# Masked query copies on GpSimd beside VectorE's PSUM reads, and query projections 40 score rows earlier, in an attention and feed-forward kernel

## Chip, cores, metric

One core of one Trainium2 chip. The metric is device time in microseconds of the whole program, the median of several runs; the lower the better. Every kernel ran in rounds with the kernel before, on the same chip in the same job; where kernels of two jobs are set against each other, their ratios to before are given. All runs used here are in the fast state. One thing still differs among fast runs, the granted TensorE clock (1.0 is full speed).

## The reference

```python
xn = layernorm(x)                                   # x: 1 x 2048 x 512, bf16
q, k, v = heads(xn @ wqkv)                          # 32 heads of 16
o = softmax(q @ k.T * 16 ** -0.5) @ v
out = x + o @ wo + (silu(xn @ w1) * (xn @ w3)) @ w2 # F = 1792
```

## The kernel before

The program is ordered when it is built. A list scheduler in the kernel has a duration for every instruction, steps time in 0.02 us, and emits work for each engine when its operands should be ready. Whatever it decides is fixed: on the chip each engine runs its own list in order and waits on semaphores. Its clock at the end of planning is called the **planned end** below: 786.0 us for the kernel before, 782.6 for the changed one. It is not a time of the chip.

Scores come in tiles of two banks of PSUM (the memory that TensorE writes; SBUF is the one that the other operands lie in), 1024 tiles in all (2048 "score rows", two per tile; a unit of queries has 64 rows). A tile's exponential is made on ScalarE, or on VectorE from a PSUM read ("p1") and four bit operations on pairs of tiles. Two units share one projected query tile: the even heads of it serve one unit, the odd heads the other, each with the rest masked to zero.

```python
def tile_QT(qc, i):
    u0 = qc * NG + 2 * i
    s0, s1 = u0 % 4, (u0 + 1) % 4                   # ring of four query slots
    ...                                             # 4 groups of projection matmuls into the "dense bank", the PSUM bank of projections and feed-forward
    def evac(bk, o, rel):
        def emit():
            q = P.op("dve", ... tensor_scalar(QT[:, s1, :], bank(bk), QS, None, ALU.mult), dur=d_cost(512))
            rel(q)
            q = P.op("dve", ... tensor_scalar(QT[:, s0, :], QT[:, s1, :], msk[:, 0:1], None, ALU.mult), dur=s_cost(512))
            done[("QTm", u0)] = q.end + _LAT        # scores of unit u0 may start
            q = P.op("dve", ... tensor_scalar(QT[:, s1, :], QT[:, s1, :], msk[:, 1:2], None, ALU.mult), dur=s_cost(512))
            done[("QTm", u0 + 1)] = q.end + _LAT
        P.post("dve", emit, ready=o.end + _LAT, prio=1)
...
crit.append((max(1, (qc * NG + 2 * i) * RPU - 60), k, tile_QT(qc, i)))   # begin 60 score rows ahead
```

GpSimd already had one job: the two 256-wide normalisation pieces of a head pair (`e5h`), which the scheduler emits beside a p1 (`beside_p1`) once their DMA should have landed.

## Time and profile before

| | |
|---|---|
| time | 798.39 us, median of 3 (798.28 to 800.65) |
| span of the profiled execution | 795.3 us, granted clock 0.996 |
| busy | ScalarE 772.0, VectorE 768.8, TensorE 750.3, GpSimd 38.0 us |
| exponential tiles | 798 on ScalarE, 226 on VectorE |
| masked copies | 30 on VectorE, 0.27 us each start to start |

The busy shares say that two engines are full; the start-to-start times in a timeline say what an instruction really costs, since neighbours overlap; the bracket at the end of a timeline line says how long the engine sat idle before it and who ended that. The lines themselves are in the prediction.

### The profile page before, as it was taken

How to read it: one execution, taken by the hardware profiler on the slowest of the kernel's cores; microseconds unless marked ns; L12 is line 12 of the kernel's file. 1: busy time of each engine (PE TensorE's matmuls, PEld its weight loads, DVE VectorE, ACT ScalarE, POOL GpSimd, SP SyncE). 2: the span in 40 equal slices, each digit the busy share in tenths (PEclk: the TensorE clock that was granted, in tenths of full speed). 3: DMA queues.
4: the chain of work that ended last, by engine and by line, in shares of the span. 5: the costliest groups of instructions: out<-in, count | busy, mean ns of one | idle time of the engine just before them, and what ended most of it. 6: DMA issues, size and time to landing. Idle time of an engine off the chain costs nothing.

```text
span 795.3 us, 21182 instructions
## 1 busy us (share of the span) xinstructions
PE 750.3 (94%) x9169; PEld 227.6 (29%) x9169; DVE 768.8 (97%) x1039; ACT 772.0 (97%) x872; POOL 38.0 (5%) x60
## 2 busy tenths in 40 slices
PE   8999999999899999999999999998999998999997
PEld 6332222222222222222222222222222222222223
DVE  8899999999999999999999999999999999999993
ACT  5999999999999999999999999999999999999994
POOL 3100201000010000000000000000100000000000
PEclk9999999999999999999999999999999999999989
DMA  7024033331322222233311234322223341332221
GB/s 213 2 23 118 5 35 42 36 34 36 48 35 30 30 36 48 34 48 53 45 17 15 37 47 59 49 33 45 28 22 36 54 60 22 51 35 23 22 15 33
DMA packets 83568, 32.91 MB, mean 41 GB/s; under 512 B 72073, under 2 KB 79753, under 8 KB 83465
## 3 DMA queue, kind: packets, MB, share of 16 engines
q1 hardware_dynamic: 83464, 31.46, 27.6%
q8 instruction: 74, 1.21, 0.6%
q14 instruction: 30, 0.24, 0.1%
HBM read 22.81 MB, written 2.10 MB: 31 GB/s over the span
## 4 chain that ended last, share of the span: by engine, by line
ACT 63%; DVE 23%; PE 12%; issue 1%; DVEq 0%; ACTq 0%
ACT f_PT L1847 60%; DVE f_xd L1920 8%; PE ps L1330 4%; DVE f_xd L1969 4%; PE ps L1784 4%; PE ps L2038 3%; DVE f_xd L1962 2%; ACT f_th L1544 2%; DVE f_xd L1978 2%; DVE f_xd L1984 2%; DVE f_hT L1558 2%; DVE f_t L1548 1%; PE ps L1217 1%; DVE f_U L2056 1%; DVE f_QT L1458 0%
## 5 line engine op out<-in xcount | busy, mean ns | idle before, releaser
L1847 ACT ACTIVATE f_PT<-ps 128x1024 bf16<-128x1024 f32 x798 | 747.6, 1138 | 4.4 <-PE ps L1784 3.7
L1784 PE MATMUL ps<-f_QT,f_KT 32*128 32x512 bf16 x2048 | 310.8, 386 | 26.6 <-ACT f_PT L1847 20.4
L1920 DVE TENSOR_SCALAR f_xd<-ps 128x1024 int16<-128x1024 f32 x226 | 275.1, 1217 | 3.0 <-PE ps L1784 2.7
L2038 PE MATMUL ps<-f_PT,f_Vaug 128*17 128x512 bf16 (+1 forms) x1596 | 210.0, 386 | 3.4 <-DVE f_U L2056 2.2
L2038 PE MATMUL ps<-f_xd,f_Vaug 128*32 128x512 bf16 (+1 forms) x1356 | 182.3, 385 | 3.9 <-DVE f_xd L1969 1.6
L1784 PEld LDWEIGHTS ps<-f_QT,f_KT 32*128 32x128 bf16 x2048 | 79.6, 91 | 323.0 <-ACT f_PT L1847 259.8
L1330 PE MATMUL ps<-f_xnT,f_w 128*32 128x512 bf16 x1792 | 139.9, 384 | 3.0 <-DVE f_t L1548 1.2
L1969 DVE TENSOR_TENSOR f_xd<-f_xd 128x2048 bf16<-128x2048 bf16 x113 | 137.3, 1215 | 0.0
L1962 DVE TENSOR_SCALAR f_xd<-f_xd 128x2048 int16<-128x2048 int16 x113 | 80.5, 713 | 2.7 <-PE ps L2038 1.9
L1984 DVE TENSOR_SCALAR f_xd<-f_xd 128x2048 int16<-128x2048 int16 x113 | 78.0, 690 | 0.0
L1978 DVE TENSOR_SCALAR f_xd<-f_xd 128x2048 int16<-128x2048 int16 x113 | 77.6, 687 | 0.0
L1330 PE MATMUL ps<-f_w,f_hT 128*32 128x512 bf16 x896 | 73.0, 383 | 0.2
L2038 PEld LDWEIGHTS ps<-f_PT,f_Vaug 128*17 128x17 bf16 (+1 forms) x1596 | 51.0, 92 | 63.7 <-issue 45.8
L2038 PEld LDWEIGHTS ps<-f_xd,f_Vaug 128*32 128x32 bf16 (+1 forms) x1356 | 44.5, 92 | 51.3 <-issue 26.9
L2100 POOL TENSOR_TENSOR f_onorm<-f_U,f_R 128x256 bf16<-128x256 f32 x30 | 25.1, 842 | 703.2 <-DMA f_R<-f_Rrow 414.0
L1330 PEld LDWEIGHTS ps<-f_xnT,f_w 128*32 128x32 bf16 x1792 | 36.8, 94 | 62.2 <-issue 51.5
L1544 ACT ACTIVATE f_th<-ps 128x512 f32<-128x512 f32 x56 | 41.0, 733 | 0.0
L1558 DVE SCALAR_TENSOR_TENSOR f_hT<-f_t,ps 128x512 bf16<-128x512 bf16 x56 | 38.0, 679 | 0.4 <-PE ps L1330 0.2
L1548 DVE SCALAR_TENSOR_TENSOR f_t<-f_th,ps 128x512 bf16<-128x512 f32 x56 | 38.0, 678 | 0.3 <-ACT f_th L1544 0.3
L1330 PEld LDWEIGHTS ps<-f_w,f_hT 128*32 128x32 bf16 x896 | 19.3, 95 | 23.7 <-issue 16.3
L2056 DVE COPY f_U<-ps 128x512 f32<-128x512 f32 x31 | 21.2, 685 | 0.4 <-PE ps L2038 0.4
L1330 PE MATMUL ps<-f_wo,f_onorm 128*32 128x512 bf16 x272 | 19.9, 382 | 0.2 <-DVE f_QT L1458 0.2
(81 smaller groups left out, 240.1 us busy)
## 6 DMA issues: line engine op xcount, KB each, us to landing
f_w<-in_B_w_dram SPq DMA_DIRECT2D x112, 128.0 KB, 3.9
f_R<-f_Rrow SPq DMA_DIRECT2D x124, 32.0 KB, 4.1
f_xr<-in_A_x_dram SPq DMA_DIRECT2D x16, 128.0 KB, 2.6
f_U<-f_U SPq DMA_DIRECT2D x60, 32.0 KB, 1.9
f_w<-in_B_w_dram SPq DMA_DIRECT2D x7, 256.0 KB
f_xd<-in_A_x_dram SPq DMA_DIRECT2D x3, 512.0 KB
out_dram<-f_xn_sb SPq DMA_DIRECT2D x12, 128.0 KB
f_xd<-in_A_x_dram SPq DMA_DIRECT2D x2, 256.0 KB
```

Source lines behind the costliest of these rows:

```text
L1330: ins = e.matmul(bank(bk)[32 * i:32 * i + 32, 0:ncols], make_lhsT(i), rhs_ap, start=start, stop=stop, tile_position=(0, 32 * i))
L1544: q = P.op("act", lambda e: e.activation(th[:, ss, :], bank(bk), ACTF.Tanh, scale=0.5), reads=[("ps", bk)], writes=[("th", ss)], dur=a_cos ...
L1548: q2 = P.op("dve", lambda e: e.scalar_tensor_tensor(t1[:, ss, :], th[:, ss, :], 1.0, bank(bk), ALU.add, ALU.mult), reads=[("th", ss), ("ps ...
L1558: q = P.op("dve", lambda e: e.scalar_tensor_tensor(hT[:, fc, :], t1[:, ss, :], 0.5, bank(bk), ALU.mult, ALU.mult), reads=[("t1", ss), ("ps ...
L1784: ins = e.matmul(bank(b), l_, r_, start=True, stop=True, tile_position=(rp, 0))
L1847: q = P.op("act", lambda e: e.activation(PT[:, s_, :], ps[:, b0 * 512:(b0 + 2) * 512], ACTF.Exp, scale=ASC, bias=ABIAS), reads=[("ps", b0) ...
L1920: q = P.op("dve", lambda e: e.tensor_scalar(dsl[:, ys, 1024 * c:1024 * c + 1024], ps[:, b0 * 512:b0 * 512 + 1024], YB, G_LO, ALU.add, ALU. ...
L1962: P.op("dve", lambda e: e.tensor_scalar(dsl[:, NY + m_, 0:n], y, 0x7F, 0x3F00, ALU.bitwise_and, ALU.bitwise_or), reads=YK, writes=[("ds", ...
L1969: q_ = P.op("dve", lambda e: e.tensor_tensor(t_ap.bitcast(BF16), y.bitcast(BF16), t_ap.bitcast(BF16), ALU.mult), reads=YK + [("ds", NY + m ...
L1978: q_ = P.op("dve", lambda e: e.tensor_scalar(g_ap, y, -G_LO, 0.0, ALU.add, ALU.max), reads=YK, writes=[("g", g_, k) for k in range(n // 51 ...
L1984: q_ = P.op("dve", lambda e: e.tensor_scalar(y, y, 0x7F80, None, ALU.bitwise_and), reads=YK, writes=YK, dur=s_cost(n), name="e", lock=True)
L2038: ins = e.matmul(bank(PV)[32 * j:32 * j + (17 if g % 2 == 0 else 32), :], v_, p_, start=s0, stop=s1, tile_position=(0, 32 * j))
```

## The change

Intent: take the two masked copies of each of 15 query tiles off VectorE and give them to GpSimd, in four pieces that run while VectorE reads PSUM and so, by the argument in the prediction, does not need the SBUF port pair that both share; start the projection earlier to leave time for that.

```diff
+    QP_DUR = 0.5
@@ tile_QT, evac
-                    q = P.op("dve", ... QT[:, s0, :] <- QT[:, s1, :] * msk[:, 0:1] ..., lock=True)
-                    done[("QTm", u0)] = q.end + _LAT
-                    q = P.op("dve", ... QT[:, s1, :] <- QT[:, s1, :] * msk[:, 1:2] ..., lock=True)
-                    done[("QTm", u0 + 1)] = q.end + _LAT
+                    P.post("pool", lambda: part(0), ready=q.end + _LAT, prio=1, cond=beside_p1)
+
+                def part(i):
+                    h, cs = i // 2, slice(256 * (i % 2), 256 * (i % 2) + 256)
+                    d_ = (s0, s1)[h]
+                    q = P.op("pool", lambda e: e.tensor_scalar(QT[:, d_, cs], QT[:, s1, cs], msk[:, h:h + 1], None, ALU.mult),
+                             reads=[("QT", s1), ("msk", h)], writes=[("QT", d_)], dur=QP_DUR, name="evQ",
+                             extra=[st["p1_op"]])
+                    if i % 2:
+                        done[("QTm", u0 + h)] = q.end + _LAT
+                    if i < 3:
+                        P.post("pool", lambda: part(i + 1), ready=q.end + _LAT, prio=1, cond=beside_p1)
@@
-                    crit.append((max(1, (qc * NG + 2 * i) * RPU - 60), k, tile_QT(qc, i)))
+                    crit.append((max(1, (qc * NG + 2 * i) * RPU - 100), k, tile_QT(qc, i)))
```

(`beside_p1` moves to where both users see it.)

More of the change, by code (lines that the diff above doesn't have):

```diff
@@ L1427, in tile_D0, with beside_p1 @@
             return out_
+        def beside_p1():
+            return st["p1_at"] == P.t
         def tile_KT(i, sc):
@@ L1460, in emit @@
                     rel(q)
-                    q = P.op("dve", lambda e: e.tensor_scalar(QT[:, s0, :], QT[:, s1, :], msk[:, 0:1], None, ALU.mult),
-                             reads=[("QT", s1), ("msk", 0)], writes=[("QT", s0)], dur=s_cost(512), name="evQ", lock=True)
-                    done[("QTm", u0)] = q.end + _LAT
-                    q = P.op("dve", lambda e: e.tensor_scalar(QT[:, s1, :], QT[:, s1, :], msk[:, 1:2], None, ALU.mult),
-                             reads=[("QT", s1), ("msk", 1)], writes=[("QT", s1)], dur=s_cost(512), name="evQ", lock=True)
-                    done[("QTm", u0 + 1)] = q.end + _LAT
+                    P.post("pool", lambda: part(0), ready=q.end + _LAT, prio=1, cond=beside_p1)
[9 more added lines that the diff above has]
+                        P.post("pool", lambda: part(i + 1), ready=q.end + _LAT, prio=1, cond=beside_p1)
                 P.post("dve", emit, ready=o.end + _LAT, prio=1)
@@ L2092, in e4 @@
                         ("OUT", (u // 2 - NON) // NP * 4 + i) in done for i in range(4))))
-            def beside_p1():
-                return st["p1_at"] == P.t
             def e5h(i):
```

## The prediction

> **What bounds the kernel now.** I read the page's busy shares first, then the forty slices, the chain that ended last, the groups of instructions, and then timelines of VectorE around one query evacuation, of ScalarE over the first 70 us and of GpSimd.
>
> The page of the kernel before:
>
> ```profile
> PE 750.3 (94%) x9169; PEld 227.6 (29%) x9169; DVE 768.8 (97%) x1039; ACT 772.0 (97%) x872; POOL 38.0 (5%) x60
> ACT 63%; DVE 23%; PE 12%; issue 1%; DVEq 0%; ACTq 0%
> L1847 ACT ACTIVATE f_PT<-ps 128x1024 bf16<-128x1024 f32 x798 | 747.6, 1138 | 4.4 <-PE ps L1784 3.7
> L1920 DVE TENSOR_SCALAR f_xd<-ps 128x1024 int16<-128x1024 f32 x226 | 275.1, 1217 | 3.0 <-PE ps L1784 2.7
> L1969 DVE TENSOR_TENSOR f_xd<-f_xd 128x2048 bf16<-128x2048 bf16 x113 | 137.3, 1215 | 0.0
> L1962 DVE TENSOR_SCALAR f_xd<-f_xd 128x2048 int16<-128x2048 int16 x113 | 80.5, 713 | 2.7 <-PE ps L2038 1.9
> L2100 POOL TENSOR_TENSOR f_onorm<-f_U,f_R 128x256 bf16<-128x256 f32 x30 | 25.1, 842 | 703.2 <-DMA f_R<-f_Rrow 414.0
> ```
>
> ScalarE and VectorE are both full, and that is by design: a score tile of 1024 columns gets its exponential either on ScalarE (798 of them) or on VectorE (226, by bit operations; 798 + 226 = 1024). The program is ordered at build time by a list scheduler with its own durations, so freed time on one engine is shared out between both by giving it more tiles. GpSimd is idle at 95%. The chain is ScalarE's exponentials for 60% of the span, with VectorE's 23% mixed in: neither engine alone sets the end. The last 16 us (output projection) contain no query work.
>
> VectorE's timeline around one of the 15 query evacuations:
>
> ```profile
> 190.41 1.22 DVE L1920 TENSOR_SCALAR f_xd<-ps 128x1024 int16<-128x1024 f32 x1
> 191.54 0.68 DVE L1458 TENSOR_SCALAR f_QT<-ps 128x512 bf16<-128x512 f32 x1
> 192.26 0.35 DVE L1461 TENSOR_SCALAR f_QT<-f_QT,f_msk 128x512 bf16<-128x512 bf16 x1
> 192.53 0.35 DVE L1464 TENSOR_SCALAR f_QT<-f_QT,f_msk 128x512 bf16<-128x512 bf16 x1
> 192.79 0.68 DVE L2056 COPY f_U<-ps 128x512 f32<-128x512 f32 x1
> 193.39 0.68 DVE L1984 TENSOR_SCALAR f_xd<-f_xd 128x2048 int16<-128x2048 int16 x1
> ```
>
> Instructions overlap, so starts count, not durations. The masked copies hold VectorE from 192.26 to 192.79. The evacuation takes 0.72 us to the next start, where the same shape without a dependent follower (L2056) takes 0.60.
>
> ScalarE's timeline (30 to 69 us), and VectorE's at the same place:
>
> ```profile
> 30.80 36.90 ACT L1847 ACTIVATE f_PT<-ps 128x1024 bf16<-128x1024 f32 x40
> 69.00 3.77 ACT L1847 ACTIVATE f_PT<-ps 128x1024 bf16<-128x1024 f32 x4 [1.30 <-PE ps L1784]
> ...
> 67.34 0.69 DVE L1458 TENSOR_SCALAR f_QT<-ps 128x512 bf16<-128x512 f32 x1 [0.75 <-PE ps L1330]
> 68.07 0.35 DVE L1461 TENSOR_SCALAR f_QT<-f_QT,f_msk 128x512 bf16<-128x512 bf16 x1
> ```
>
> This is the one place where queries are late. VectorE sat idle 0.75 us for the first query projection, and ScalarE sat idle 1.30 us until scores of the unit using it came. The 40 exponentials also give ScalarE's cost: (36.90 - 1.14) / 39 = 0.917 us per tile.
>
> GpSimd's timeline against VectorE's, where a normalisation piece came late:
>
> ```profile
> 179.35 0.72 POOL L2100 TENSOR_TENSOR f_onorm<-f_U,f_R 128x256 bf16<-128x256 f32 x1 [45.40 <-DVE f_xd L1920]
> 181.30 0.73 POOL L2100 TENSOR_TENSOR f_onorm<-f_U,f_R 128x256 bf16<-128x256 f32 x1 [1.22 <-DVE f_hT L1558]
> ...
> 179.38 1.25 DVE L1962 TENSOR_SCALAR f_xd<-f_xd 128x2048 int16<-128x2048 int16 x1
> 180.55 0.67 DVE L1558 SCALAR_TENSOR_TENSOR f_hT<-f_t,ps 128x512 bf16<-128x512 bf16 x1
> 181.15 1.21 DVE L1920 TENSOR_SCALAR f_xd<-ps 128x1024 int16<-128x1024 f32 x1
> ```
>
> The piece at 179.35 fell beside a 16-bit SBUF operation, whose 0.69 became 1.25. The piece at 181.30 fell 0.15 after the start of a PSUM read (L1920), which stayed at 1.21.
>
> **What the Trainium skill says.** "SBUF — State Buffer", section "Who interferes with whom": VectorE in a 2-port mode contends with GpSimd and whoever issues first blocks the other for the whole instruction, while a VectorE instruction with at most one SBUF input outside these modes does not. The pair of pieces above agrees: +0.56 us in one case, nothing in the other. "VectorE: DVE Perf Modes", section "Why PSUM operands drop a tier", says the 2-port mode is impossible with a PSUM operand, which is why the change pairs its pieces with the PSUM reads. "GPSIMD Engine Reference", section "3.1 Elementwise — side-by-side cycle accounting", gives 1.03 to 1.8 cycles per element at 1.2 GHz for one-input loops; before has no such piece of this width, only a 2-column scalar operation of 0.19 us. "Perfetto Trace Analysis", section "GPSIMD Engine Instruction", calls a GpSimd span in a profile unreliable; I use the spans only to see whether a piece fits beside a read.
>
> **The change part by part.**
>
> Removed: two masked copies in each of 15 query tiles. Start to start, 1.25 us from the evacuation to the instruction after the copies (192.79 - 191.54) becomes the usual 0.60, so 0.65 us per tile, 15 x 0.65 = 9.8 us of VectorE. The scheduler's durations for the two copies are 0.21 us each (its formula: 0.075 + 0.000261 x 512); it knows of 15 x 0.42 = 6.3 us. The other 3.5 us (dependence wait and longer copies) are lateness of the real VectorE against the plan.
>
> Worth of VectorE time: a pair of VectorE tiles costs two PSUM reads at 1.13, three 16-bit operations at 0.60 and one product at 1.13 (all start to start), 5.19 us, or 2.60 per tile. Rates are 1/0.917 = 1.09 tiles per us on ScalarE and 1/2.60 = 0.385 on VectorE, 1.475 together. One microsecond freed on VectorE yields 0.385 tiles, 0.385/1.475 = 0.26 us of span. The planned 6.3 us give 1.6 us. The unplanned 3.5 us give between 0.26 and 1 us each, depending on whether they now delay ScalarE through PE's fixed order: 0.9 to 3.5; I take 1.7. About two exponentials should move to VectorE.
>
> Added: 60 GpSimd pieces of 128x256 bf16. Estimate from the skill's cycles and the 0.19 us of the small operation: 256 x 1.03 / 1200 + 0.19 = 0.41 to 256 x 1.8 / 1200 + 0.19 = 0.57 us, total 25 to 34 us on an idle engine. Each waits for the VectorE instruction in front of a PSUM read, so it should start about 0.15 after the read and end by 0.72, inside its 1.13. Aligned pieces cost VectorE nothing.
>
> Misalignment: GpSimd runs in order, and the existing normalisation pieces wait for a DMA that lands later than planned (the page lists 414 us of idle ended by it; the group's R loads take 4.1 us to land). Eight 16-bit operations are stretched over the nominal 0.69 in before's timeline, by about 3.6 us together. New query evacuations come about 15 us earlier (40 rows at 2048 rows in 770 us = 2.66 per us), around 132, 176, 226 us, and their pieces spread over some four reads, about 10 us; normalisation pieces at 131, 179, 231 us fall within these stretches. So perhaps 5 to 10 query pieces queue behind a late one and each may block VectorE for 0.2 to 0.4 us: 1 to 3 us, of which I charge 1.0 to the span.
>
> Moved: the projections start 100 rather than 60 rows ahead, 38 us instead of 23 us at that rate. The four pieces need around 10 us, so they are ready in time. The old queries of the four-slot ring were used up 128 rows ahead, so the ring allows it. For the first tile the old place in the order of the single dense PSUM bank was behind V and K tiles and just too late; now it comes early. I expect ScalarE's 1.30 us of idle there to go: 1.2 us.
>
> Sum: 1.6 + 1.7 + 1.2 - 1.0 = 3.5 us. From 798.4 that is 794.9. As a re-planned greedy order falls a little better or worse by chance, and all chances to lose are outside the planner, I put 795.4.
>
> **The rivals.** First, VectorE alone is the bound: all 9.8 us come off, 788.6. Against it: ScalarE is at 99.9 of 100 us in most windows and carries 60% of the chain. Second, the port: a majority of pieces misaligned, 60 x 0.4 = 24 us of VectorE blocked, cancelling the gain and giving 800 to 806. Against it: most second normalisation pieces, which wait for VectorE alone, land on their reads. Third, a new wait: PE held by late GpSimd copies at unit boundaries. At 20 us or more of slack this costs nothing; if GpSimd were jammed, the span would go to 800. Fourth, PE at 94%: every tile moved to VectorE brings three product groups where ScalarE's brings one, and the earlier projections crowd the one dense bank; then the gain shrinks to 1 us, 797.
>
> **Range and chances.** 795.4 with 792.4 to 798.8 eight times in 10: the low end has the unplanned 3.5 us fully returned and a lucky order, the high end has the gain eaten by blocked ports. Two per cent is 16 us; even the first rival gives 1.2%. Faster 0.01, same 0.98, slower 0.01.
>
> **What would show it.** Right: no masked copies on VectorE and evacuations followed after 0.60 us; 60 GpSimd pieces at 0.4 to 0.6 us starting just after the start of PSUM reads; ScalarE without idle time near 68 us; 796 or so exponentials and 228 PSUM reads; stretched 16-bit operations still under about 15. Wrong: many stretched 16-bit operations, PE's score loads waiting for GpSimd, a ScalarE sum of idle time over before's, or a fall near 10 us, which would mean the sharing factor of 0.26 is wrong.

## The result

The changed kernel took 791.24 us (790.52 to 792.25, 4 runs) against 798.34 us of before (797.80 to 800.65, 4 runs): ratio 0.9907, 95% interval 0.9883 to 0.9930. A second job on another chip gave 790.93 against 797.54 us, ratio 0.9916. A ratio is the mean time of one kernel's fast runs over that of the other's of the same rounds, so not quite the ratio of the medians. So 7 us are gained where I had put 3, and 791.24 lies under the range. It is still within 2%.

The page of the changed kernel, to be held against the page lines of before in the prediction:

```profile
PE 747.2 (95%) x9177; PEld 223.6 (28%) x9177; DVE 763.5 (97%) x1015; ACT 768.5 (97%) x870; POOL 90.4 (11%) x120
ACT 80%; PE 11%; DVE 8%; issue 1%; DMA 0%; POOL 0%; DVEq 0%; ACTq 0%
L1857 ACT ACTIVATE f_PT<-ps 128x1024 bf16<-128x1024 f32 x796 | 745.1, 1161 | 3.8 <-PE ps L1794 3.6
L1930 DVE TENSOR_SCALAR f_xd<-ps 128x1024 int16<-128x1024 f32 x228 | 277.2, 1216 | 2.3 <-PE ps L1794 1.8
L1470 POOL TENSOR_SCALAR f_QT<-f_QT,f_msk 128x256 bf16<-128x256 bf16 x60 | 55.4, 923 | 271.7 <-DVE f_xd L1988 112.3
```

Two exponential tiles moved from ScalarE to VectorE, as foreseen, and the 60 pieces are there. VectorE's share of the chain fell from 23% to 8%: it now holds ScalarE up less often. Each piece takes 0.92 us, not my 0.41 to 0.57.

A timeline of the changed kernel, GpSimd and VectorE at one query tile:

```profile
182.94 1.21 DVE L1930 TENSOR_SCALAR f_xd<-ps 128x1024 int16<-128x1024 f32 x1
183.12 0.92 POOL L1470 TENSOR_SCALAR f_QT<-f_QT,f_msk 128x256 bf16<-128x256 bf16 x1 [3.35 <-DVE f_xd L1994]
184.08 0.67 DVE L1558 SCALAR_TENSOR_TENSOR f_t<-f_th,ps 128x512 bf16<-128x512 f32 x1
184.67 0.68 DVE L1988 TENSOR_SCALAR f_xd<-f_xd 128x2048 int16<-128x2048 int16 x1
```

The piece starts 0.18 us after the PSUM read and ends at 184.04, just before the next VectorE instruction: by its span, which the profile gives only roughly on GpSimd, it fits with 0.04 us to spare. The 16-bit operation after it has its normal 0.68.

ScalarE from 30 us on, in the changed kernel:

```profile
30.36 50.52 ACT L1857 ACTIVATE f_PT<-ps 128x1024 bf16<-128x1024 f32 x55
```

The 1.30 us idle at 69 us is gone.

None of this explains 7 us. The plan says 3.4 (786.0 to 782.6). To see where the rest is, I ran the scheduler by itself and set the start of every exponential on ScalarE in the trace against its planned start. The difference is the *lateness*; if it grows, the chip lost time that the plan does not know of. Beside it stands the sum by which VectorE's SBUF operations were stretched over their usual duration (0.69 for the 16-bit ones, 1.22 for the products and reads), counted over all of a trace's instructions from 30 us on, where it is over 0.06 us; outside the two untied kernels and the wide one below, what overlapped was a normalisation piece.

| trace | lateness at planned 66 us | at 730 us | growth | stretched VectorE operations |
|---|---|---|---|---|
| before | 0.50 | 4.04 | 3.5 | 8, 3.5 us |
| changed | -0.02 | 1.44 | 1.5 | 7, 1.5 us, none beside a query piece |

So before loses 2 us more than the changed kernel on its way to 730 us, and the stretched operations have about the same difference (one of before's eight, 0.4 us, comes later). This is where the experiments start. The theories: (1) the plan, 3.4 us; (2, "P") blocking of VectorE by normalisation pieces, which fell by accident of the new order; (3, "Q") queries that come earlier take out hidden waits; (4, "H") the granted TensorE clock, found later.

### The profile page after: what moved, and what is told of

It is laid out like the page before. It is cut to its first block, busy times and chain, and to the rows that moved or that the text cites. A ratio compares the mean times of both kernels' runs of the same rounds, so it can differ in the third digit from the quotient of the medians.

```text
span 790.5 us, 21316 instructions
## 1 busy us (share of the span) xinstructions
PE 747.2 (95%) x9177; PEld 223.6 (28%) x9177; DVE 763.5 (97%) x1015; ACT 768.5 (97%) x870; POOL 90.4 (11%) x120
## 3 DMA queue, kind: packets, MB, share of 16 engines
q8 instruction: 74, 1.21, 0.6%
## 4 chain that ended last, share of the span: by engine, by line
ACT 80%; PE 11%; DVE 8%; issue 1%; DMA 0%; POOL 0%; DVEq 0%; ACTq 0%
ACT f_PT L1857 76%; PE ps L1331 4%; PE ps L1794 3%; ACT f_th L1554 3%; DVE f_xd L1930 3%; PE ps L2048 2%; DVE f_xd L1979 1%; DVE f_xd L1994 1%; DVE f_xd L1988 1%; DVE f_xd L1972 1%; DVE f_hT L1568 0%; DVE f_t L1558 0%; DMA f_xd<-in_A_x_dram 0%; PE ps L1343 0%; DVE f_stats L1255 0%
## 5 line engine op out<-in xcount | busy, mean ns | idle before, releaser
L1794 PE MATMUL ps<-f_QT,f_KT 32*128 32x512 bf16 x2048 | 314.0, 385 | 25.1 <-ACT f_PT L1857 19.0
L2048 PE MATMUL ps<-f_PT,f_Vaug 128*17 128x512 bf16 (+1 forms) x1592 | 202.8, 384 | 1.1 <-DVE f_U L2066 0.5
L2048 PE MATMUL ps<-f_xd,f_Vaug 128*32 128x512 bf16 (+1 forms) x1368 | 179.0, 384 | 5.5 <-DVE f_U L2066 3.8
L1331 PE MATMUL ps<-f_xnT,f_w 128*32 128x512 bf16 x1792 | 142.2, 384 | 3.7 <-DVE f_t L1558 1.8
L1979 DVE TENSOR_TENSOR f_xd<-f_xd 128x2048 bf16<-128x2048 bf16 x114 | 139.3, 1222 | 0.0
L1470 POOL TENSOR_SCALAR f_QT<-f_QT,f_msk 128x256 bf16<-128x256 bf16 x60 | 55.4, 923 | 271.7 <-DVE f_xd L1988 112.3
L1331 PE MATMUL ps<-f_wo,f_onorm 128*32 128x512 bf16 x272 | 21.8, 408 | 0.2 <-DVE f_wkv L1613 0.2
```

The lines of the kernel that those rows point to most:

```text
L1331: ins = e.matmul(bank(bk)[32 * i:32 * i + 32, 0:ncols], make_lhsT(i), rhs_ap, start=start, stop=stop, tile_position=(0, 32 * i))
L1470: q = P.op("pool", lambda e: e.tensor_scalar(QT[:, d_, cs], QT[:, s1, cs], msk[:, h:h + 1], None, ALU.mult), reads=[("QT", s1), ("msk", h) ...
L1794: ins = e.matmul(bank(b), l_, r_, start=True, stop=True, tile_position=(rp, 0))
L1979: q_ = P.op("dve", lambda e: e.tensor_tensor(t_ap.bitcast(BF16), y.bitcast(BF16), t_ap.bitcast(BF16), ALU.mult), reads=YK + [("ds", NY + m ...
L2048: ins = e.matmul(bank(PV)[32 * j:32 * j + (17 if g % 2 == 0 else 32), :], v_, p_, start=s0, stop=s1, tile_position=(0, 32 * j))
```

## The experiments

lead_only, nocopy100, pool_free and pool_lead60 were made to part the change (lead, copies, tie to the PSUM reads), the others to find what the plan does not contain. For all: 5 rounds, medians, ratio to before with its interval. All results were correct but one.

### after_again: the changed kernel again

> The changed kernel once more, to size the gain on the chip that also runs its parts. Theory 1 (planned gain plus lateness): the program's own list scheduler, run when the kernel is built, plans an end at 786.0 us before and 782.6 after, so 3.4 us are planned; the measured 7.1 us contain 3.7 us of something the plan does not know, and the repeat should show about 7 again (ratio 0.990 to 0.992). Rival (noise): the profiled pair of executions differed by only 4.8 us of span, and the repeat should show about 4.8 (ratio 0.994).

790.93 us against 797.54, ratio 0.9916 (0.9895 to 0.9936): 6.6 us. The gain stands; the smaller difference of the profiled pair was the luck of two executions. Theory 1 alone falls short by about 3 us.

### lead_only: the earlier start alone

```diff
 before
-  ... * RPU - 60), k, tile_QT(qc, i)))
+  ... * RPU - 100), k, tile_QT(qc, i)))
```

> The kernel before with query projections begun 100 instead of 60 rows ahead and nothing else; the masked copies stay on VectorE. Planned end 784.9, 1.1 us under before. Theory A (the lead removes the one stall near 68 us): 1.1 to 1.3 us faster, ScalarE's idle of 1.30 us gone. Theory B (earlier queries take out small hidden waits everywhere): 3 to 5 us faster. Theory C (moving is worth nothing on the chip): 0.

792.62 us, ratio 0.9940 (0.9920 to 0.9961): 4.9 us faster with all masked copies still on VectorE. That is theory B's number, and I had given the lead 1.2 us. ScalarE's timeline (30 to 90 us) shows the idle time at 69 us gone:

```profile
30.53 60.60 ACT L1847 ACTIVATE f_PT<-ps 128x1024 bf16<-128x1024 f32 x66 [0.21 <-PE ps L1784]
```

But lateness grows by 1.4 us here, against 3.5 in before, and 5 stretched operations sum to 1.0 us, against 3.5. So "hidden waits for queries" is not the only reading: the new order also happened to place the normalisation pieces better. Copies on GpSimd add 1.7 us to this (792.62 to 790.93); the plan has 2.3 for them and I had 1.6.

### nocopy100: no masked copies at all (wrong result)

```diff
 lead_only
-  q = P.op("dve", ... both masked copies ...)
+  done[("QTm", u0)] = done[("QTm", u0 + 1)] = q.end + _LAT
@@ score()
-  QT[32 * j:32 * j + 32, u % 4, :]
+  QT[32 * j:32 * j + 32, (u | 1) % 4, :]        # from u = 2 on
```

> Lead 100 and the masked copies done by nobody (wrong result on purpose: both units of a pair read the unmasked queries). Its plan for TensorE, ScalarE and VectorE is that of the changed kernel, end 782.6; only the 60 GpSimd pieces are missing. Theory 1 (aligned pieces are free): the same time as the changed kernel within 1 us. Rival (pieces of 0.92 us, longer than I estimated, still block VectorE now and then): 1 to 4 us faster than the changed kernel.

792.19 us (ratio 0.9925, 0.9904 to 0.9946), relative error 1.17. It is no faster than the changed kernel; the lower mean clock of its runs (0.997 against 0.998) is worth some 0.6 us at most by the slope given under "The clock". So the 60 pieces cost VectorE nothing measurable: my charge of 1.0 us for query pieces that block VectorE was wrong.

### pool_free: query pieces not tied to PSUM reads

```diff
 changed
-  P.post("pool", lambda: part(0), ready=q.end + _LAT, prio=1, cond=beside_p1)
+  P.post("pool", lambda: part(0), ready=q.end + _LAT, prio=1)
-  ..., name="evQ", extra=[st["p1_op"]])
+  ..., name="evQ")
```

> The changed kernel with the pieces no longer tied to PSUM reads: the four of a tile run on GpSimd as soon as the evacuation is done. The planned order of the other engines is again the same (782.6). If the port is what the tie is for, about three of four pieces fall beside 16-bit operations or products on VectorE and each blocks it for 0.3 to 0.9 us: 45 x 0.5 = 22 us of VectorE, of which the static order passes on at least half, so 8 to 20 us slower than the changed kernel. If contention is small or absorbed: less than 2 us slower.

793.16 us (ratio 0.9938, 0.9915 to 0.9960), 2.2 us slower than the changed kernel. The tie is worth that at most, not the 8 to 20 us that I expected: the mean clock of these runs was 0.996 against 0.998, worth about 0.9 us by the slope given under "The clock". The timeline of this kernel shows why:

```profile
126.95 3.83 POOL L1470 TENSOR_SCALAR f_QT<-f_QT,f_msk 128x256 bf16<-128x256 bf16 x2
127.91 1.22 DVE L1978 TENSOR_TENSOR f_xd<-f_xd 128x2048 bf16<-128x2048 bf16 x1
129.05 0.69 DVE L1971 TENSOR_SCALAR f_xd<-f_xd 128x2048 int16<-128x2048 int16 x1
129.65 0.89 DVE L1993 TENSOR_SCALAR f_xd<-f_xd 128x2048 int16<-128x2048 int16 x1
```

VectorE has its SBUF operations back to back here, and it is GpSimd that waits: two pieces take 3.83 us instead of 1.8, and VectorE loses 0.20. Over the whole trace 27 of the 60 pieces take longer than 1 us, 22 us more in sum than at 0.92 each, while twenty stretched VectorE operations, some of them beside normalisation pieces, sum to only 4.3 us.

### norm_late: before, with its normalisation pieces placed later

```diff
 before
-  P.post(eng, e5h(0) or e5, ready=q.end + _LAT + (R_LAG if eng == "dve" else 0.0), ...)
+  P.post(eng, e5h(0) or e5, ready=q.end + _LAT + (R_LAG if eng == "dve" else 2.5), ...)
```

Where such a piece waits for its DMA in before, it starts 2.6 to 6.2 us later than planned, and so misses the read that it was planned beside. Only GpSimd's list changes; the plans of TensorE, ScalarE, VectorE and the DMA queue are identical to before's.

> The kernel before, with one change: the GpSimd normalisation pieces are tied to a PSUM read planned 2.5 us later than the planned landing of their DMA (the real landing is 2 to 6 us later than planned). The planned order of TensorE, ScalarE, VectorE and of the DMA queue is identical to before (end 786.0); query copies and lead stay as before. Theory P (the unplanned part of the gain is port blocking by normalisation pieces, eight stretched VectorE operations with 3.5 us in before against five with 1.0 us in the lead-only kernel): stretched operations fall to at most 3 with under 1 us, and the kernel is 2 to 3.5 us faster than before. Rival Q (the unplanned part comes from queries being earlier): the same time as before within 0.7 us.

795.28 us against 798.57, ratio 0.9955 (0.9942 to 0.9969): 3.3 us. No stretched operation is left, and lateness grows by 1.1 us between 66 and 730 us, where before has 3.5. Theory P holds; rival Q falls. As to the size: 2.4 of the 3.3 us are the smaller growth of lateness, and a part of the rest may be the clock, which was 0.994 in these runs and 0.992 in those of before in this job. The same place in both timelines, before first:

```profile
562.45 2.40 POOL L2100 TENSOR_TENSOR f_onorm<-f_U,f_R 128x256 bf16<-128x256 f32 x2 [48.99 <-DMA f_R<-f_Rrow]
563.04 1.22 DVE L1962 TENSOR_SCALAR f_xd<-f_xd 128x2048 int16<-128x2048 int16 x1
564.19 1.21 DVE L1984 TENSOR_SCALAR f_xd<-f_xd 128x2048 int16<-128x2048 int16 x1
```

and norm_late:

```profile
563.42 1.22 DVE L1920 TENSOR_SCALAR f_xd<-ps 128x1024 int16<-128x1024 f32 x1
563.59 0.73 POOL L2100 TENSOR_TENSOR f_onorm<-f_U,f_R 128x256 bf16<-128x256 f32 x1 [48.69 <-DVE f_t L1548]
564.56 0.69 DVE L1978 TENSOR_SCALAR f_xd<-f_xd 128x2048 int16<-128x2048 int16 x1
```

In before the pieces waited for the DMA and fell beside 16-bit operations, which took 1.22 and 1.21 instead of 0.69. In norm_late they wait for VectorE's instruction in front of a PSUM read, which comes later than the DMA, and nothing is stretched.

### after_norm_late: the same in the changed kernel

```diff
 changed
-  ... (R_LAG if eng == "dve" else 0.0)
+  ... (R_LAG if eng == "dve" else 1.5)
```

> The changed kernel with its normalisation pieces tied 1.5 us later; the planned order of the other engines is identical to the changed kernel (end 782.6). Theory P: its 1.5 us of stretched operations (all beside normalisation pieces, none beside query pieces) fall to under 0.7 and it is 0.7 to 1.5 us faster than the changed kernel. Rival (blocking in the changed kernel is absorbed): no difference. Candidate for the best version.

791.86 us, ratio 0.9903 (0.9887 to 0.9920). By the ratio it is level with the changed kernel (0.9907 and 0.9916), not faster. 5 operations remain stretched, by 0.85 us in sum. A miss: the 0.7 us less of blocking does not show over the scatter of the clock (0.992 to 0.999 in its runs; their mean of 0.996 against 0.998 alone would hide it).

### norm_untied: the opposite

```diff
 changed
-  cond=lambda: (eng == "dve" or beside_p1()) and (...)
+  cond=lambda: (...)
-  ..., dur=0.72, extra=[st["p1_op"]])      # and cond=beside_p1 of the second piece
+  ..., dur=0.72)
```

> The changed kernel with the normalisation pieces (two-input, 0.73 us) no longer tied to PSUM reads; the query pieces stay tied, and the planned order of the other engines is identical. Theory P (these pieces, not the query pieces, block VectorE): its stretched VectorE operations rise from 1.5 us to 4 us or more and the time by 1.5 to 4 us. Rival (GpSimd mostly waits for VectorE, not the other way about, as in the kernel with untied query pieces): under 1 us slower.

792.64 us (ratio 0.9927, 0.9913 to 0.9940), 0.9 to 1.6 us slower than the changed kernel by the ratios. 24 stretched operations sum to 4.5 us, three times the changed kernel's sum. 11 of them stand beside query pieces alone, which run behind the late normalisation pieces in GpSimd's order and can so miss their reads. The sign is theory P's, the size at its low end or under it.

### after_lead108: eight rows more

```diff
 changed
-  ... * RPU - 100), k, tile_QT(qc, i)))
+  ... * RPU - 108), k, tile_QT(qc, i)))
```

> The changed kernel with the projections 108 instead of 100 rows ahead. Eight more rows have no meaning for any wait, but the list scheduler's order happens to end at 785.1 us instead of 782.6. Theory (the chip follows the plan, and a part of any gain is the luck of the order): 1.5 to 3.5 us slower than the changed kernel. Rival (the plan's last microseconds don't show on the chip): within 1 us.

794.12 us, ratio 0.9941 (0.9928 to 0.9954). That gives away 2.0 to 2.7 us of the gain by the ratios, at a clock that is no lower (0.997 to 1.0). The planned end is 2.5 us later, and 7 operations are stretched by 3.2 us, which is 1.7 more than in the changed kernel; the two together are not seen in full. The chip follows the order, and the order is a lottery of some microseconds: with lead 100 the change drew well. (It also sits at an edge: planned again with 95 to 99 rows the changed kernel locks up, with 104 it has the planned end of 100.)

### pool_lead60: copies on GpSimd alone

```diff
 changed
-  return st["p1_at"] == P.t
+  return st["p1_at"] == P.t or P.free["dve"] <= P.t - 0.3
-  ... * RPU - 100), k, tile_QT(qc, i)))
+  ... * RPU - 60), k, tile_QT(qc, i)))
```

> The GpSimd copies alone, with the lead left at 60 rows. As the change has it this cannot be built at a lead of 95 rows or less: the plan locks up, since the last copies of a pair wait for a PSUM read beside which to run and all scores before them are spent. So a piece may also run where VectorE has been idle in the plan for 0.3 us. Planned end 786.2, no better than before. If the copies' 6.3 us of planned VectorE time are worth their 2 us wherever they come: 2 us faster than before. If the copies coming later than on VectorE make new waits at pair borders that eat it: within 1 us of before or slower, with ScalarE's exponentials or TensorE's score loads waiting near 68 us by over 2 us.

796.75 us, ratio 0.9977 (0.9964 to 0.9989): 1.8 us. That is not the worth of the copies, since the plan has no gain (786.2 against 786.0): lateness grew by 2.0 us against 3.5 in before, and the mean clock was 0.995 against before's 0.992 in this job. The masked copies of the first query tile are done later than in before, and ScalarE waits twice:

```profile
68.92 0.49 ACT L1525 ACTIVATE f_Vaug<-ps 128x384 bf16<-128x384 f32 x1 [1.27 <-PE ps L1515]
70.70 20.27 ACT L1857 ACTIVATE f_PT<-ps 128x1024 bf16<-128x1024 f32 x22 [1.29 <-PE ps L1794]
```

The earlier start is thus not only a gain in itself: as written, the copies on GpSimd can't be planned with a lead of 95 rows or less.

### copies_more: 8 us of VectorE time that the plan does not know

```diff
 before
+  for k_ in range(2):
+      e.tensor_scalar(scr[:, k_, :], QT[:, s1, :], msk[:, 0:1], None, ALU.mult)
   e.tensor_scalar(QT[:, s0, :], QT[:, s1, :], msk[:, 0:1], None, ALU.mult)
```

> The kernel before with two more masked copies per query tile, written to a scratch tile and unknown to the plan: 30 more VectorE instructions of 0.27 us start to start, 8 us of real VectorE time in a planned order that is identical to before on every engine. It measures the factor of my prediction for unplanned VectorE time (0.26 to 1 of span per us; I had taken 1.7 us for 3.5). If unplanned time is passed on whole: 8 us slower than before. If the sharing factor held: 2 us. If lateness of half a us at a time is caught up by slack between VectorE and its readers: under 1 us.

806.33 us against 798.09, ratio 1.0104 (1.0086 to 1.0122): 8.2 us for 8 us. Time added to VectorE behind the plan's back is passed on nearly whole; lateness grows by 10.5 us, 7.0 more than in before, in steps at the query tiles. The factor of 0.26 holds only for time that the scheduler knows and can share out.

### pool_wide: pieces of 512 columns

```diff
 changed
-  h, cs = i // 2, slice(256 * (i % 2), 256 * (i % 2) + 256)
+  h, cs = i, slice(0, 512)                      # two pieces per tile instead of four; QP_DUR = 0.9
```

> The changed kernel with each masked copy as one piece of 512 columns, 30 instead of 60; same planned order elsewhere. A piece should take about 1.75 us (2 x 0.92 less a fixed 0.1), longer than the 1.13 us of the PSUM read beside it, so its end falls on the next VectorE operation. If the piece keeps the port: 30 x 0.5 us = 15 us of stretched operations and 5 to 12 us slower. If VectorE's operation or the piece slips with little loss: under 2 us slower, and the width of 256 is not what counts.

793.59 us, ratio 0.9943 (0.9930 to 0.9956): 2.1 to 2.9 us slower by the ratios. A piece takes 1.56 us, more than the read:

```profile
375.74 1.21 DVE L1930 TENSOR_SCALAR f_xd<-ps 128x1024 int16<-128x1024 f32 x1
375.98 1.56 POOL L1470 TENSOR_SCALAR f_QT<-f_QT,f_msk 128x512 bf16<-128x512 bf16 x1 [3.04 <-DVE f_xd L1994]
376.98 1.11 DVE L1972 TENSOR_SCALAR f_xd<-f_xd 128x2048 int16<-128x2048 int16 x1
```

The 16-bit operation after the read takes 1.11 instead of 0.69. Only 15 operations are stretched, 5.3 us in sum, 9 of them beside query pieces; in 9 of 30 cases the VectorE instruction after the read is another PSUM read, and none of these is stretched. The width of 256 is right, and it is close: 0.92 us in a read of 1.13.

### best_try: the lowest plan of 240

```diff
 changed
-    VBS = 5
+    VBS = 6
-    PVQ = 28
+    PVQ = 24
 lead 110, normalisation pieces 2.5 us later
```

> A try at a better version: the changed kernel with lead 110, normalisation pieces tied 2.5 us later, and two knobs of the list scheduler moved (V tiles 6 rows apart instead of 5, product backlog 24 instead of 28), the lowest planned end of 240 variants: 782.0 against 782.6 (the middle of the 188 that could be planned at all is 785.2, so the changed kernel lies near the low end). Expected from the plan 0.6 us and from the later ties up to 1 us: 0.5 to 1.6 us faster than the changed kernel, 789.5 to 790.5. If the order brings more blocking or other lateness: within 1 us of it or slower.

790.18 us, ratio 0.9906 (0.9886 to 0.9925). One operation is stretched, by 0.3 us, and the fastest run (789.09) is a microsecond under the changed kernel's. By the ratio it is level with the changed kernel.

### The clock: before_warm, norm_late_warm, after_nl_warm, best_warm

All 53 timed runs of before in these jobs had a mean clock of 0.989 to 0.997 (mean 0.993), and by a line through them they get slower by 0.5 us for each thousandth that the clock is lower. The changed kernel's 10 runs had 0.994 to 1.0 (mean 0.998). (A run at 0.998 need not have lost anything: in after_again's trace this mean comes from half clock in the last 2.5 us alone, after TensorE's work.) Stretches of the trace show where the clock went; before, from 760.8 to 778 us:

```profile
core 0: us, PE busy (x) PEld busy (x) DVE busy (x) ACT busy (x) POOL busy (x), PEclk, DMA share, GB/s
760.80:764.30 3.50, 3.04 (x30) 0.81 (x28) 3.50 (x5) 3.50 (x5) 0.00 (x0) 1.00 0.02 2
764.30:767.70 3.40, 2.25 (x26) 0.73 (x22) 3.33 (x7) 3.40 (x5) 0.00 (x0) 1.00 0.04 7
767.70:771.10 3.40, 3.40 (x24) 0.68 (x22) 3.40 (x5) 3.40 (x4) 0.00 (x0) 0.54 0.78 29
771.10:774.50 3.40, 3.40 (x26) 0.69 (x22) 3.27 (x4) 2.74 (x4) 0.00 (x0) 0.50 0.38 48
774.50:778.00 3.50, 3.50 (x46) 1.19 (x40) 3.50 (x6) 3.50 (x5) 0.00 (x0) 0.96 0.00 0
```

At 764 us there are no feed-forward tiles left to fill TensorE between the last scores (26 matmuls in 3.4 us, where 46 run at 774.5). Then its clock is halved for 6.8 us, and ScalarE, which was full, sits idle (2.74 of 3.40). The Trainium skill, "TensorE: Matmul & The Clock Gate", section "What's actually happening", describes a monitor that sets the clock to full or half by how busy the array has been, in free-running stretches of 3413 ns. In these traces the 14 halved stretches inside the run last one, two or three times 3.413 us, and each begins right after such a stretch with low activity, 39 to 52% by counting for every matmul 0.217 us, the distance of two matmul starts in a row here, and merging overlaps. What it costs is seen in the lateness. Between planned 765 us and the last exponential it grows by 1.0 us in before, 1.7 in norm_late and 2.4 in the profiled run of the changed kernel, where 6.8 us are halved; in lead_only and after_again, where nothing is halved there, by 0.1 us or less. To test it, scores in the low were issued twice:

```diff
@@ score()
+  if any(a_ <= P.t < b_ for a_, b_ in WARM_AT):  # 750 to 772 us; in the changed order also 301 to 309
+      mms = mms + mms
```

(best_warm has 629 to 638 and 752 to 772.)

> The kernel before with each pair of score matmuls planned between 750 and 772 us issued twice (the result is the same, since the second pair overwrites the first); the planned order of all engines is identical. Theory H (low TensorE activity in a 3.413 us stretch halves its clock for the next): the mean clock rises from 0.993 to 0.997 or more and the kernel is 1.5 to 3 us faster than before although it does more work. Rival (the clock falls for another cause, such as power or chance): clock as before, and the 0.22 us that each score comes later makes it 0 to 3 us slower.

797.35 us, ratio 0.9990 (0.9975 to 1.0004), clock 0.996 to 1.0. The clock rose, so activity is the cause. The time did not fall: each score's signal comes later by the second pair, and lateness grows by 1.5 us from planned 730 to 765 us, where before has no growth.

> Before's planned order with both disturbances taken out: normalisation pieces tied later, and the low of TensorE near the end filled. Theory H and P together: clock 0.997 or more, no stretched VectorE operations, 791.5 to 793.5 us of time, 1 to 2.5 us faster than norm_late alone (795.3). Rival: the same as norm_late or slower.

795.35 us, ratio 0.9961 (0.9948 to 0.9974), all six clocks 0.999 or 1.0, and the runs lie within 0.5 us of each other. Clock as expected, time not (lateness again grows by 1.5 us from 730 to 765).

> The changed kernel's planned order with both disturbances taken out (later ties, lows near 305 us and near the end filled). If all of the gain beyond the plan was blocking and clock, norm_late_warm minus this is the planned 3.4 us, within 1 us: 788 to 790 us. If the change brings something else besides, the difference stays over 5.

793.20 us, ratio 0.9935 (0.9922 to 0.9949), clock 0.999 or 1.0, runs within 0.5 us. A miss by over 3 us (lateness grows by 2.1 us from 730 to 765). It is 2.2 us under norm_late_warm, but with one more filled low, so no clean test.

> The best version so far (planned end 782.0) with its lows near 633 us and near the end filled in the same way. 788 to 789.5 us with a clock of 0.998 or more, 1 to 2 us under the changed kernel. If filling delays scores more than it saves: 790 to 792.

795.56 us, ratio 0.9967 (0.9949 to 0.9985): 5 us worse than best_try. Nothing is halved at the two filled places, but the trace has a new low and a halved stretch of two lengths at about 735 us, and lateness grows by 5.6 us from 730 to 765. A failure, and its cause was not followed further.

### The closing pair: norm_late_fill and after_nl_fill

To fill without delaying, one matmul is put *behind* the score's own signal, into the dense bank while that is idle. Nothing waits for it.

```diff
@@ score(), after the score pair's P.op
+  if any(a_ <= P.t < b_ for a_, b_ in WARM_AT) and idle((6,)):
+      z_ = _Prog.op(P, "pe", lambda e: e.matmul(bank(6), KT[0:32, ...], QT[0:32, ...], start=True, stop=True, ...),
+                    reads=rd, writes=[("ps", 6)])
```

> Before's planned order with later ties and the low of TensorE near the end filled by one matmul behind each score pair, into the dense bank while it is idle; nothing waits for it. If the clock is worth time: clock 0.997 or more, and 792.5 to 794 us (the fit of norm_late's runs over the clock gives a span of 791.7 at full clock, 793.5 of time), 1.5 to 3 us faster than norm_late's 795.3. If filling costs as much as it gives again: 795 or more.

794.02 us against 798.02, ratio 0.9954 (0.9941 to 0.9968), clock 0.998 to 1.0.

> The changed kernel's order, later ties, lows near 305 us and near the end filled in the same way. If the gain is the plan's 3.4 us plus blocking plus clock: 3.4 us under norm_late_fill within 1 us, 789 to 790.5 us, with a spread of its runs under 1.5 us, and so level with or slightly better than the changed kernel (791). If something else is in the gain: more than 5 us under norm_late_fill.

790.79 us, ratio 0.9913 (0.9900 to 0.9927), clock 0.998 to 1.0. The two differ by 3.2 us, where the plans differ by 3.4. The stretch that was halved in before, in norm_late_fill:

```profile
764.30:767.70 3.40, 3.01 (x27) 0.75 (x27) 3.19 (x5) 3.40 (x5) 0.00 (x0) 1.00 0.67 26
767.70:771.10 3.40, 3.14 (x33) 0.88 (x31) 3.40 (x5) 3.40 (x5) 0.00 (x0) 1.00 0.48 51
```

TensorE is at full clock, and ScalarE stays nearly full.

So with blocking and clock taken out of both orders (0.8 us of stretching is left in after_nl_fill), what is left of the gain is the planned part. In one job, on one chip: 798.02 to 794.02 is what before lost to blocking and clock (4.0 us, 3.7 by the ratio), 794.02 to 790.79 is the better order (3.2 us), and 790.79 is where the changed kernel is without any repair (791.24 and 790.93 in its own jobs). One thing stays open here: the changed kernel still has 1.5 us of stretching and in some runs a halved clock, yet repairing both brought nothing that shows by the ratios (0.9913 against 0.9907 and 0.9916).

## Why the prediction was wrong, by its own steps

**Worth of planned VectorE time** (6.3 us by 0.26 gives 1.6): right. The plan has 2.3 for it (784.9 of the lead alone to 782.6), the chip 1.7. Two tiles changed engine, as said. The sharing factor must not be used for time that the plan does not know: copies_more passed on 7 to 8.2 us for 8.

**Lead** (1.2 us for the stall near 68 us): right in the mechanism, the idle time is gone, and the plan has 1.1. But the chip gave 4.9 for the lead alone. The rest is not a property of the lead, but of the order that came out with it: stretched operations fell from 3.5 to 1.0 us and the mean clock rose from 0.993 to 0.998.

**Misalignment**, the step that failed ("1 to 3 us, of which I charge 1.0 to the span"): the sign was wrong. I saw the eight stretched operations in before and asked only what the new pieces would add to them. They added none: not one of the 60 stretches anything, and leaving them out gained nothing. The old normalisation pieces, which I took as a fixed cost, were moved by the new order: 1.5 us of stretching instead of 3.5. Taking that cost out of before, with nothing else changed, gave 3.3 us, of which 2.4 show as lateness that went away with the stretching. I had these 3.6 us in hand as a number, and treated them as background.

**Unplanned 3.5 us of the old copies** (taken as 1.7): not found. norm_late has these copies on VectorE and no blocking, and its lateness grows by 1.1 us; after_nl_fill has no such copies and grows by 1.2 with 0.8 us of stretching. Why 8 further us pass on nearly whole while these do not show is open; slack of about 0.2 us per query tile between the plan's durations and the real ones would do it, but no run tests that.

**A term that was missing: TensorE's clock.** The prediction has no word on it, though the page of before shows an 8 among the nines of the clock row. At 0.5 us per thousandth, 0.993 against 0.998 is 2.7 us as an upper estimate; the fill that removes it brought 1.3 us by the medians of two jobs (795.28 to 794.02), but nothing by the ratios (0.9955 and 0.9954). The traces are clearer: after planned 765 us the lateness grows by 1.7 us in norm_late and by 0.2 in norm_late_fill. So the clock was worth about 1.5 us in that profiled run, and its mean over all runs is not known better than 0 to 1.3 us.

**Duration of a piece**: 0.92 us instead of my 0.41 to 0.57. It did no harm, because a piece starts 0.18 us after a read of 1.13 us; pool_wide shows what a longer one costs.

Of the rivals, the crowded port did not come. The new wait at unit borders did not come with the lead of 100 rows (TensorE's weight loads waited for query pieces 0.4 us, once), and came with 60 (1.3 us, in three waits). The gain was not shrunk to 1 us by a crowded TensorE either. The first rival, VectorE alone, gives 788.6 and is nearer to the measured time than my own number, for a wrong reason.

## What to carry to other kernels

When a program's order is fixed at build time, compare planned with real start times before and after a change: a growing lateness is time that the plan does not know, and a re-planned order changes it by accident, in either direction. Disturbances found in the old trace (here eight stretched operations and a halved clock) belong into the sum of a prediction as something that the change may remove. And tie a GpSimd piece to the event that really comes last: beside a PSUM read it cost nothing, while pieces let loose by a late DMA cost before 2.4 to 3.3 us.

## What the Trainium skill lacked or had wrong

- "GPSIMD Engine Reference", section "3.1 Elementwise — side-by-side cycle accounting", has 1.03 to 1.8 cycles per element for one-input loops, and nothing on this instruction. By its span in the profile a bf16 multiplication by a per-partition scalar took here 0.922 us for 256 and 1.562 us for 512 columns: (1.562 - 0.922) / 256 = 2.5 ns, 3 cycles of 1.2 GHz per element, and 0.28 us fixed.
- "SBUF — State Buffer", section "Who interferes with whom", says that whoever issues first blocks the other. It lacks what this comes to where VectorE's operations follow each other closely: GpSimd loses most. Two loose pieces took 3.83 us instead of 1.84, and VectorE's operation beside them 0.89 instead of 0.69; in the whole of pool_free 22 us against 4.3.
- "TensorE: Matmul & The Clock Gate", section "What's actually happening", names an idle stretch as what halves the clock; elsewhere the page tells of frequent short idles doing it too, but it gives no share of activity. Here stretches with 39 to 52% of activity were enough (by the count given above), though not every stretch under 52% was followed by a halving, and filling the one near 764 us brought the clock from 0.992 to 0.999 (before and before_warm).
